# Decay attention with a softplus feed-forward block: value products of batches 1 to 7 in float32 on two column tiles

## The chip, the cores and the metric

The kernel runs on one core of a Trainium2 chip. The metric is the device time of one execution in microseconds. Three runs of the kernel before took 1167.11, 1168.81 and 1170.86 us; the median is 1168.81.

## The reference

For each of 8 batches and 8 heads there are 576 queries, keys and values of width 64, all float32, and a row of 576 forget factors f.

```python
scores = scale * np.matmul(q, k.transpose(0, 1, 3, 2))
cum = np.cumsum(np.log(np.clip(f, 0.0001, 1.0)), axis=-1)
scores = np.where(causal, -1000000000.0, scores + cum[..., :, None] - cum[..., None, :])
attn = np.exp(scores - np.max(scores, axis=-1, keepdims=True))
attn = attn / (np.sum(attn, axis=-1, keepdims=True) + 1e-09)
x = np.matmul(attn, v)          # then (B, H, S, D) -> (B*S, H*D) = (4608, 512)
h = x @ w_in                    # (512, 2048)
out = (np.maximum(h, 0.0) + np.log1p(np.exp(-np.abs(h)))) @ w_out   # (2048, 512)
```

The mask leaves a query only the keys up to its own place, so a product of the softmax with the values runs, for a group of 128 keys, over the queries from that group on.

## The kernel before

The work is a list of operations (class Plan). Each has the engines on which it may run with a cost for each, the operations that it waits for, and the buffers that it takes. Plan.run walks the list once, when the program is built: it always takes the operation that can start first by these costs, on the engine that would finish it first, and so writes out a fixed order for each engine's queue. All DMAs but a few are issued from SP's queue. A change of a cost, a buffer count or a dependence changes the whole order.

The attention is done head by head (the function attention). Batch 0 comes first, in 14 jobs of its own shapes, called plain; then 56 jobs made by whole(b, h), one for each head of batches 1 to 7. Between the units of a job, units of the feed-forward block (FFN) of earlier tokens are added, and after the last head the rest of the FFN runs alone. FFN products at L1205 (up) and L1290 (down) split each operand into a rounded high part and a low part (type float32r) and use three products for one; those of the first 256 tokens (L1186, L1309) are plain float32.

A whole job has these steps. Scores: two float32r products for each piece (L794, L795), from an operand T that four small DMAs put together. A row minimum on DVE (L799), an exponential on ACT that also sums the rows (L827), then a scaling by the reciprocal sum on ACT, POOL or DVE (L855, L857). The softmax is transposed on TensorE (L922), 128 keys by up to 512 queries in a bank of PSUM, in four banks of a head: bank 0 holds the first 64 queries against keys 0 to 63 and the last 64 queries against the last 64 keys (small), bank 1 the queries from 64 against keys 0 to 127, bank 2 those from 128 against the next 128 keys, bank 3 the rest.

Before the change, hi_part copies a bank to float32r (ph; a copy's line is L215), and lo_part subtracts that from the bank (pl, L944; L941 for the small bank, whose low part goes to partitions 64 to 127). split_v does the same to the values (vhl, cast and L723), high and low part side by side, so that one 128-column stationary operand gives both products in PSUM partitions 0 to 63 and 64 to 127. output(gi) then makes the value products (L1055): one of 64 columns for the first 64 queries, and nine for queries 64 to 575 (512, 448, 320 and 192 columns with ph and with pl, and one of 64). The two halves of the result are added in two steps: ACT copies one half into x (shift), DVE adds the other (put, L1081).

For the plain jobs there is output_tiled (L995): float32 products from one float32 copy of the transposed softmax and from V as it was loaded, with 64 stationary columns each. Each product goes to one of two column tiles of TensorE (tile_position (0, 0) or (0, 64)), which write PSUM partitions 0 to 63 and 64 to 127, and the two tiles take different ranges of queries. A float32 product is two records in the trace, one for each pass. For a rest job (one head of batch 0, queries 256 to 575) the ranges are 256 to 447 and 448 to 575.

Of the kernel before, what the change touches and what calls it, by code (L numbers as in the profile page):

```python
# [218 lines left out]
def tile_decay_attention_softplus_ffn(  # L219
# [38 lines left out]
    BUFS = dict(T=2, att=4, h=2, acc=2, fe=4, ph=3, pl=3, ph64=2, gh=LAG + 1, gl=LAG + 1, xh=1, xl=1,  # L258
                x32=2, wl=2, vhl=3, vraw=1, raw=2, one=2)
# [40 lines left out]
    PW = [64] + [128 * (i + 1) for i in range(1, 5)]  # L300
# [252 lines left out]
    def whole(b, h):  # L553


        banks = [[(0, 0, 64, 0, NCH), (512, 512, S, 0, 4)], [(0, 64, S, 0, 0)], [(128, 128, S, 0, 1)],
                 [(256, 256, S, 0, 2), (384, 384, S, 0, 3)]]
        return dict(
            b=b, heads=[h], q=(0, S), k=(0, S), nv=NCH + 1,
            tiles=[(q0, n, 0, i, 0) for i, (q0, n) in enumerate(QT)],  # L560
            banks=banks, groups=[(0, 64, h, 0), (64, S, h, 64)],
        )
# [41 lines left out]
    def attention(job):  # L604
# [33 lines left out]
        def load_v(pairs=(None,)):  # L638
            for h in pairs:
                box, vtag = {}, "vraw"  # L640
                if plain:
                    vtag = ("vhl", "vhl", "vraw", "vhl")[slot if h is None else h // 2]

                def v(e, h=h, box=box, vtag=vtag):
                    shape = [P, (NCH + 1) * (2 if vtag == "vhl" else 1), D]
                    vr = box["v"] = buf(vtag, shape, f"vr{n}")[:, 0:nv]
                    if h is not None:
                        e.dma_start(
                            out=vr[:, 0:4].rearrange("p (h c) d -> p h c d", h=2),
                            in_=vR[b, h : h + 2, :, 0:2].rearrange("h p c d -> p h c d"),  # L650
                        )
                    else:
                        e.dma_start(out=vr[:, 0:NCH], in_=vR[b, heads[0]])
# [6 lines left out]
                more = (160, 1) if plain else (192, 2)  # L660
                if h is not None:
                    more = 128, 1
                later = first_rows if plain and h is None else []
                op = add_dma(v, *more, after=later, takes=(vtag,))
                st.setdefault("vr", []).append(box)
                st.setdefault("V", []).append(op)
                st["vtag"] = vtag
                if h is not None:
                    V_of[h] = [box], [op], vtag
# [46 lines left out]
        def split_v():  # L716
            def v_hi(e):
                st["vhl"] = buf("vhl", [P, nv, 2 * D], f"vhl{n}", F32R)
                copy(e, st["vhl"][:, 0:nv, 0:D], st["vr"][0]["v"])

            def v_lo(e):
                hi, lo = st["vhl"][:, 0:nv, 0:D], st["vhl"][:, 0:nv, D : 2 * D]
                e.tensor_sub(lo, st["vr"][0]["v"], hi.bitcast(F32))  # L723

            vh = add(
                [on_act(nv * D), on_dve(nv * D, bias=COPY_BIAS)], v_hi, after=st["V"], takes=("vhl",),
            )
            vl = add(subs(nv * D), v_lo, after=[vh])
            give("vraw", [vl])
            st["V"] = [vl]  # L730

        def prepare():
# [20 lines left out]
            split_v()  # L753
# [113 lines left out]
        def weights(bi):  # L867
# [6 lines left out]
            small = spans[0][:3] == (0, 0, 64)  # L874
            blocks, need = [], []
            for ti, (q0, n_q, k0, pi, po) in enumerate(tiles):
                for key, lo, hi, _, at in spans if small else reversed(spans):
                    if q0 < hi and q0 + n_q > lo and k0 <= key:
# [6 lines left out]
                        if small:  # L885

                            x = pt[pi][:, c : c + 64]
                            one = halves
                            if key == 0:

                                x, one = x[0:68], ident[0:68, 0:68]
# [34 lines left out]

            def keep(e):
# [3 lines left out]
            more, size = ("64", P) if small else ("", 512)  # L931
            rows = 64 if small else P

            def hi_part(e):
                box["h"] = buf("ph" + more, [P, size], f"ph{n}_{bi}", F32R)[:, 0:w]
                copy(e, box["h"][0:rows], box["ps"][0:rows, 0:w])

            def lo_part(e):
                if small:
                    h = box["h"]  # L940
                    e.tensor_sub(h[64:P], box["ps"][0:64, 0:w], h[0:64].bitcast(F32))  # L941
                    return
                box["l"] = buf("pl", [P, size], f"pl{n}_{bi}", F32R)[:, 0:w]
                e.tensor_sub(box["l"], box["ps"][:, 0:w], box["h"].bitcast(F32))  # L944
# [11 lines left out]
            if plain:  # L956
                tag = tags[bi] = ("ph", "pl")[count["p"] % 2]
                count["p"] += 1
                ready = [add(on, keep, after=[m], takes=(tag,))]
                give("att", ready)  # L960
            else:
                hp = add(on, hi_part, after=[m], takes=("ph" + more,))
                ready = [hp, add(on_dve(w), lo_part, after=[hp], takes=() if small else ("pl",))]
                give("att", ready[1:])
            for key, lo, hi, vc, at in spans:
                parts.append((lo, hi, bi, vc, at, box, ready, small))

        def output_tiled():

            steps = [[] for _ in banks]  # L970
            for gi, (g0, g1, r, c0) in enumerate(groups):
                todo = [x for x in parts if x[0] < g1 and x[1] > g0]
                todo.sort(key=lambda x: (max(x[0], g0) > g0, x[2]))
                for lo, hi, bi, vc, at, pbox, ready, _ in todo:
# [3 lines left out]
                        ready=ready,  # L978
                    )
                    steps[bi].append(mm)  # L980
# [6 lines left out]
            for i, step in enumerate(steps):  # L987
# [24 lines left out]
            for r, rows, c, w, bi, o, h, tok in job["puts"]:  # L1012
# [17 lines left out]
            if quad:  # L1030
                s_of[heads[0]] = s_of[heads[2]] = st["scores"], before
            else:
                scores, reads = s_of[heads[0]] if pair else ([], [])
                give("T0", st["scores"] + scores)
                give(st["vtag"], before + reads)
# [4 lines left out]

        def output(gi):
            g0, g1, h, tok = groups[gi]
            g, j = h // 2, h % 2
            todo = sorted(
                (p for p in parts if p[0] < g1 and p[1] > g0), key=lambda p: (max(p[0], g0) > g0, p[2])
            )
            box, last = {}, []
            for i, (lo, hi, bi, vc, at, pbox, ready, small) in enumerate(todo):
                a, z = max(lo, g0), min(hi, g1)

                def values(e, i=i, a=a, z=z, vc=vc, o=at + a - lo, pbox=pbox, xs="h" if small else "hl"):
                    if i == 0:
                        box["ps"] = bank("att", f"o{n}_{gi}")
                    for x in xs:
                        e.matmul(  # L1055
                            box["ps"][:, a - g0 : z - g0], st["vhl"][:, vc[1], :],
                            pbox[x][:, o : o + z - a],
                            start=i == 0 and x == "h", stop=i == len(todo) - 1 and x == xs[-1],
                        )

                on = on_pe(z - a, len("h" if small else "hl"))
                op = add(
                    on, values, after=ready + last + st["V"],
                    takes=("att",) if i == 0 else (),
                )
                last = [op]
                used[bi].append(op)
            st.setdefault("ends", []).extend(last)
            w = g1 - g0


            def to():
                if b not in x_of:
                    x_of[b] = buf("x32", [P, NCC, S], f"x32_{b}")
                return x_of[b][64 * j : 64 * j + 64, g, tok : tok + w]

            def shift(e):
                copy(e, to(), box["ps"][64 - 64 * j : 128 - 64 * j, 0:w])

            def put(e):  # L1080
                e.tensor_add(to(), box["ps"][64 * j : 64 * j + 64, 0:w], to())  # L1081

            needs = last + x_taken.get(b, [])
            takes = () if b in x_taken else ("x32",)
            c = add(on_act(w, psum=True), shift, after=needs, takes=takes)
            d = add(on_dve(w), put, after=[c])
            x_taken.setdefault(b, [c])
            puts = [d]
            wrote.setdefault(b, []).append((tok, tok + w, d))
            give("att", puts)  # L1090
            if gi == len(groups) - 1:
                give("T", st["scores"])
                give("vhl", st["ends"])
                for bi, ops in used.items():
                    if banks[bi][0][:3] == (0, 0, 64):
                        give("ph64", ops)
# [526 lines left out]
```

## Time and profile before

| | before |
|---|---|
| runs, us | 1167.11, 1168.81, 1170.86 |
| profiled execution: span, us | 1169.7 (the page gives no other time of it) |
| TensorE (PE) busy | 1156.0 us, 99% |
| its weight loads (PEld) busy | 958.5 us, 82% |
| DVE busy | 800.1 us, 68% |
| ACT busy | 835.0 us, 71% |
| POOL busy | 136.5 us, 12% |

A group of instructions is named by its line, engine, operation and out<-in. Its busy time counts each instruction from its start to its end; matmuls are pipelined and overlap, so what a matmul takes from TensorE is read from its start to the start of the next. Idle time is shown with the instruction before which it stands and what released it. Roughly, batch 0 takes the first 130 us, the heads of batch 1 the time to 240 us, those of batches 2 to 7 the time to 980 us, and the FFN alone the rest.

### The profile page before, as it was taken

The numbers are of one execution on the slowest core, as the hardware profiler recorded it, in microseconds if no ns is written. First come the engines' busy times: TensorE is split into PE (matmuls) and PEld (weight loads), VectorE is DVE, ScalarE is ACT, GpSimd is POOL, SyncE is SP. The second block draws the span as 40 slices with busy tenths as digits, with TensorE's granted clock in tenths as the row PEclk, the third lists the DMA queues.
The fourth block names the chain that finished last, engine by engine and source line by source line (L and its number), as shares of the span: only waits on it lengthen the run. The fifth ranks groups of instructions, "written<-read, shape, count | busy, mean of one in ns | idle before, by whom it ended". The sixth has DMA issues, their size and how long they took to land.

```text
span 1169.7 us, 19392 instructions
## 1 busy us (share of the span) xinstructions
PE 1156.0 (99%) x6236; PEld 958.5 (82%) x6236; DVE 800.1 (68%) x1991; ACT 835.0 (71%) x1987; POOL 136.5 (12%) x149
## 2 busy tenths in 40 slices
PE   8999999999999999999999999999999999999998
PEld 6667788888888888888888888888888888888887
DVE  7898998987776778667876777677866772223322
ACT  6789888888867877678767786787867873444543
POOL 3323111100111101011011001110011100000000
PEclk9999999999999999999999999999999999999999
DMA  8968775555566547655566557554656433211211
GB/s 237 258 181 244 200 205 149 134 171 164 156 196 187 154 133 205 173 158 171 153 172 186 162 146 207 175 152 137 192 164 187 120 113 121 78 54 37 90 54 36
DMA packets 119397, 181.75 MB, mean 155 GB/s; under 512 B 20816, under 2 KB 78448, under 8 KB 119296
## 3 DMA queue, kind: packets, MB, share of 16 engines
q1 hardware_dynamic: 119128, 180.37, 53.3%
q8 instruction: 50, 0.82, 0.3%
q14 instruction: 51, 0.42, 0.1%
q10 hardware_dynamic: 168, 0.15, 0.0%
HBM read 110.49 MB, written 36.83 MB: 126 GB/s over the span
## 4 chain that ended last, share of the span: by engine, by line
PE 78%; DVE 9%; DMA 5%; ACT 4%; issue 2%; SPq 1%; POOL 0%; DVEq 0%; ACTq 0%; POOLq 0%
PE acc L1290 30%; PE h L1205 28%; PE b L922 7%; PE o L1055 6%; PE s L795 3%; PE s L794 3%; DMA T<-T 3%; DVE s L799 2%; ACT p L827 1%; DMA gl_5b<-g_d 1%; DVE wol_dt_float32r L538 1%; DVE xl L1157 1%; DVE woh_dt_float L470 1%; DVE vhl L723 1%; DMA sto<-in_w_out 0%
## 5 line engine op out<-in xcount | busy, mean ns | idle before, releaser
L1205 PE MATMUL h<-xh,wih 128*128 128x512 f32 (+1 forms) x576 | 229.9, 402 | 0.0
L827 ACT ACTIVATE p<-s,negm 128x288 f32<-128x288 f32 (+7 forms) x384 | 183.0, 479 | 58.0 <-DVE negm L799 53.8
L1205 PE MATMUL h<-xl,wih 128*128 128x512 f32 (+1 forms) x576 | 216.5, 379 | 0.0
L799 DVE CUSTOM_DVE_ANT_0 s<-s,cmask 128x288 f32<-128x288 f32 (+6 forms) x320 | 138.2, 438 | 90.2 <-PE s L795 83.3
L857 POOL TENSOR_SCALAR p<-p,rsum 128x448 f32<-128x448 f32 (+4 forms) x89 | 97.4, 1102 | 754.4 <-DVE rsum L841 401.4
L1252 DVE SCALAR_TENSOR_TENSOR h<-h,e 128x512 f32<-128x512 f32 x136 | 95.8, 704 | 130.1 <-ACT e L1244 129.1
L1238 ACT ACTIVATE e<-h 128x512 f32<-128x512 f32 x144 | 85.8, 596 | 119.0 <-PE h L1205 117.9
L1290 PE MATMUL acc<-woh_dt_float32r,gh 128*128 128x512 f32 x376 | 153.0, 407 | 0.0
L1205 PE MATMUL h<-xh,wl 128*128 128x512 f32 (+1 forms) x576 | 148.8, 380 | 0.0
L1290 PE MATMUL acc<-woh_dt_float32r,gl 128*128 128x512 f32 x376 | 147.3, 392 | 0.0
L1290 PE MATMUL acc<-wol_dt_float32r,gh 128*128 128x512 f32 x376 | 146.9, 391 | 0.0
L944 DVE TENSOR_TENSOR pl<-b,ph 128x512 fp32r<-128x512 f32 x168 | 111.3, 666 | 34.2 <-ACT ph L215 30.8
L215 ACT CAST ph<-b 128x512 fp32r<-128x512 f32 (+2 forms) x173 | 82.8, 482 | 56.3 <-PE b L922 51.5
L1205 PEld LDWEIGHTS h<-xh,wl 128*128 128x128 f32 x576 | 104.9, 188 | 21.6
L922 PE MATMUL b<-ident,p 128*128 128x128 f32 (+1 forms) x728 | 118.8, 269 | 2.8 <-ACT p L827 1.0
L1205 PEld LDWEIGHTS h<-xh,wih 128*128 128x128 f32 x576 | 108.8, 189 | 15.3 <-issue 0.2
L1260 DVE TENSOR_TENSOR gl<-h,gh 128x512 fp32r<-128x512 f32 x136 | 93.5, 687 | 40.2 <-ACT gh L215 39.1
L1205 PEld LDWEIGHTS h<-xl,wih 128*128 128x128 f32 x576 | 108.9, 189 | 14.4 <-issue 0.2
L922 PEld LDWEIGHTS b<-ident,p 128*128 128x128 f32 (+1 forms) x728 | 86.3, 138 | 18.8 <-ACT p L827 4.8
L215 ACT CAST gh<-h 128x512 fp32r<-128x512 f32 x114 | 66.9, 587 | 45.1 <-DVE h L1252 41.5
L794 PE MATMUL s<-T 128*64 128x64 f32 x336 | 97.3, 302 | 1.0 <-PE o L1055 0.7
L795 PE MATMUL s<-T 68*64 68x64 f32 x336 | 97.7, 295 | 0.0
(163 smaller groups left out, 2216.1 us busy)
## 6 DMA issues: line engine op xcount, KB each, us to landing
wl<-wil_d SPq DMA_DIRECT2D x72, 512.0 KB
T<-T SPq DMA_DIRECT2D x224, 144.0 KB
raw<-in_qkT SPq DMA_DIRECT2D x112, 144.0 KB
g_d<-gh SPq DMA_DIRECT2D x84, 128.0 KB
g_d<-gl SPq DMA_DIRECT2D x84, 128.0 KB
vr<-in_vR SPq DMA_DIRECT2D x64, 160.0 KB
out<-ob SPq DMA_DIRECT2D x35, 256.0 KB
sto<-in_w_out SPq DMA_DIRECT2D x11, 512.0 KB
```

Of the source, the lines that this page charges most:

```text
L215: (e.tensor_copy if hasattr(e, "tensor_copy") else e.copy)(out, in_)
L794: e.matmul(o, qA[:, q0:end], kA[:, a:z], start=True, stop=False)
L795: e.matmul(o, qB[0:ST, q0:end], kB[0:ST, a:z], start=False, stop=True)
L799: e.tensor_tensor_reduce(out=box["o"], in0=box["o"], in1=cmask[0:n_q, right - w : right], scale=-0.125, scalar=m0 if i else 3.0e38, op0=AL ...
L827: e.activation(o, box["o"], AF.Exp, bias=m1, scale=-1.0, accum_out=acc)
L857: e.tensor_scalar(a, a, f_, None, ALU.mult)
L922: e.transpose(box["ps"][0 : x.shape[1], at : at + one.shape[1]], x, one)
L944: e.tensor_sub(box["l"], box["ps"][:, 0:w], box["h"].bitcast(F32))
L1205: e.matmul(o, l, r, start=m == 0, stop=m == 11)
L1252: e.scalar_tensor_tensor(h, h, 0.0, box["e"], ALU.max, ALU.add)
L1260: e.tensor_sub(box["l"], box["t"], box["h"].bitcast(F32))
L1290: e.matmul(st["acc", tt], l, r[fc], start=first and m == 0, stop=last and m == 2,)
```

## The change

Jobs made by whole use output_tiled too. The transposed softmax is kept once, in float32 (keep), V is not split, and the queries are in two groups, 0 to 383 on the first tile and 384 to 575 on the second. The small blocks are 68 wide instead of 64, so that the products take 68 rows, of which four are zero in the softmax. The result is copied from PSUM to x in two pieces, on ACT or DVE. output, split_v, hi_part and lo_part go. Buffers: six for the transposed softmax (pt) in place of three ph and three pl, two small ones (pt64) as before, four of V (vr) in place of three vhl and one vraw.

```diff
-    BUFS = dict(T=2, att=4, h=2, acc=2, fe=4, ph=3, pl=3, ph64=2, gh=LAG + 1, gl=LAG + 1, xh=1, xl=1,
-                x32=2, wl=2, vhl=3, vraw=1, raw=2, one=2)
+    BUFS = dict(T=2, att=4, h=2, acc=2, fe=4, pt=6, pt64=2, gh=LAG + 1, gl=LAG + 1, xh=1, xl=1,
+                x32=2, wl=2, vr=4, raw=2, one=2)
...
-    PW = [64] + [128 * (i + 1) for i in range(1, 5)]
+    PW = [ST] + [128 * (i + 1) for i in range(1, 5)]
...
-        banks = [[(0, 0, 64, 0, NCH), (512, 512, S, 0, 4)], [(0, 64, S, 0, 0)], [(128, 128, S, 0, 1)],
+        banks = [[(0, 0, 64, 0, 0), (512, 512, S, 0, 4)], [(0, 64, S, 0, 0)], [(128, 128, S, 0, 1)],
...
-            banks=banks, groups=[(0, 64, h, 0), (64, S, h, 64)],
+            banks=banks, groups=[(0, 384, 0, 0), (384, S, 1, 0)],
+            puts=[(0, 384, h, 0), (64, S - 384, h, 384)],
...
-                    if nv > NCH:
-
-                        x = vR[b, heads[0], 0:64, 0]
-                        twice = bass.AP(x.tensor, x.offset, [[0, 2], *x.ap])
-                        e.dma_start(out=vr[:, NCH], in_=twice)
...
-        def split_v():
...
             def keep(e):
-                box["p"] = buf(tag, [P, 512], f"p{n}_{bi}", F32R)[:, 0:w].bitcast(F32)
-                copy(e, box["p"], box["ps"][:, 0:w])
+                rows = ST if small else P
+                box["p"] = buf(tag, [P, P if small else 512], f"p{n}_{bi}")[:, 0:w]
+                copy(e, box["p"][0:rows], box["ps"][0:rows, 0:w])
...
-                hp = add(on, hi_part, after=[m], takes=("ph" + more,))
-                ready = [hp, add(on_dve(w), lo_part, after=[hp], takes=() if small else ("pl",))]
-                give("att", ready[1:])
+            ready = [add(on, keep, after=[m], takes=(tag,))]
+            give("att", ready)
...
-                    steps[bi].append(mm)
+                    steps[bi if plain else 0].append(mm)
...
                         e.matmul(
                             box["ps"][m["r"] : m["r"] + 64, m["a"] : m["z"]],
-                            st["vr"][m["vc"][0]]["v"][:, m["vc"][1], :],
-                            m["p"]["p"][:, m["o"] : m["o"] + m["z"] - m["a"]],
+                            st["vr"][m["vc"][0]]["v"][0 : m["rows"], m["vc"][1], :],
+                            m["p"]["p"][0 : m["rows"], m["o"] : m["o"] + m["z"] - m["a"]],
                             start=m["start"], stop=m["stop"], tile_position=(0, m["r"]),
                         )
...
+            for r, w, h, tok in [] if plain else job["puts"]:
+
+                def put(e, r=r, w=w, h=h, tok=tok):
...
+                    copy(e, to, box["ps"][r : r + 64, 0:w])
...
+                on = [on_act(w, psum=True), on_dve(w)]
+                d = add(on, put, after=before + x_taken.get(b, []), takes=takes)
...
-        def output(gi):
...
-            o=[output_tiled] if plain else [lambda gi=gi: output(gi) for gi in range(len(groups))],
+            o=[output_tiled],
```

## Rows read from the trace of the kernel before

**Rows 1.** The page's part 1 with its head: busy time, share of the span and instructions of each engine.

```profile
span 1169.7 us, 19392 instructions
...
PE 1156.0 (99%) x6236; PEld 958.5 (82%) x6236; DVE 800.1 (68%) x1991; ACT 835.0 (71%) x1987; POOL 136.5 (12%) x149
```

**Rows 2.** The page's part 4, the chain of work that ended last, by engine.

```profile
PE 78%; DVE 9%; DMA 5%; ACT 4%; issue 2%; SPq 1%; POOL 0%; DVEq 0%; ACTq 0%; POOLq 0%
```

**Rows 3.** The table of stretches: from and to, length, then busy time (and instructions) of PE, PEld, DVE, ACT and POOL, the granted TensorE clock, DMA share, GB/s.

```profile
120.00:150.00 30.00, 28.92 (x183) 21.53 (x182) 28.72 (x78) 25.93 (x68) 4.20 (x3) 1.00 0.75 213
150.00:180.00 30.00, 29.36 (x194) 25.78 (x195) 27.31 (x75) 26.98 (x71) 6.37 (x5) 1.00 0.66 183
180.00:210.00 30.00, 29.09 (x189) 25.50 (x188) 26.59 (x74) 25.69 (x69) 3.54 (x3) 1.00 0.58 157
210.00:240.00 30.00, 29.77 (x183) 26.07 (x183) 27.21 (x75) 24.74 (x65) 5.45 (x5) 1.00 0.47 122
...
480.00:600.00 120.00, 120.00 (x645) 101.81 (x644) 89.85 (x223) 92.23 (x227) 12.13 (x12) 1.00 0.60 174
```

**Rows 4.** Instructions of TensorE in order of time, around the value products of two heads: start, duration, line, operation, out<-in, shape, count.

```profile
181.22 0.28 PE L1055 MATMUL o<-ph,vhl 128*128 128x64 f32 x1
181.33 0.47 PE L1290 MATMUL acc<-woh_dt_float32r,gh 128*128 128x512 f32 x1
181.65 0.39 PE L1290 MATMUL acc<-wol_dt_float32r,gh 128*128 128x512 f32 x1
181.88 0.40 PE L1290 MATMUL acc<-woh_dt_float32r,gl 128*128 128x512 f32 x1
...
272.21 0.19 PE L1055 MATMUL o<-ph,vhl 128*128 128x64 f32 x1
272.25 0.41 PE L922 MATMUL b<-halves,p 128*128 128x128 f32 x2
272.50 0.49 PE L922 MATMUL b<-ident,p 128*128 128x128 f32 x3
...
276.11 0.40 PE L1055 MATMUL o<-ph,vhl 128*128 128x512 f32 x1
...
277.47 0.28 PE L1055 MATMUL o<-pl,vhl 128*128 128x192 f32 x1
277.58 0.41 PE L1205 MATMUL h<-xh,wih 128*128 128x512 f32 x1
277.84 0.39 PE L1205 MATMUL h<-xl,wih 128*128 128x512 f32 x1
```

**Rows 5.** The same view in batch 0: FFN products without (101.06) and with (112.79) a tiled value block behind them, the block of one rest job (113.74), and the FFN products after it.

```profile
101.06 1.02 PE L1309 MATMUL acc<-wol_dt_float,g 128*128 128x512 f32 x2
101.92 1.14 PE L789 MATMUL s<-T 66*128 66x288 f32 x4
...
112.79 1.02 PE L1309 MATMUL acc<-wol_dt_float,g 128*128 128x512 f32 x2
113.74 1.31 PE L995 MATMUL o<-p,vr 128*64 128x192 f32 x18
114.98 1.98 PE L1309 MATMUL acc<-wol_dt_float,g 128*128 128x512 f32 x4
116.80 3.73 PE L1186 MATMUL h<-x,woh_dt_float 128*128 128x128 f32 x32
```

**Rows 6.** The instructions of L995: durations in ns as minimum/median/maximum, first and last start in us, the commonest shapes.

```profile
L995 PE MATMUL o<-p,vr x192: 219/273/377, 15.6 to 127.8; 128*64 128x128 f32 x112, 128*64 128x192 f32 x48, 128*64 128x64 f32 x32
```

**Rows 7.** Groups of instructions of the whole span: count, then busy us, mean ns of one, and the idle time before them with its releasers.

```profile
L944 DVE TENSOR_TENSOR pl<-b,ph 128x512 fp32r<-128x512 f32 x168 | 111.3, 666 | 34.2 <-ACT ph L215 30.8
L1081 DVE TENSOR_TENSOR x<-o,x 64x64 f32<-64x64 f32 x112 | 50.7, 452 | 12.5 <-ACT x L215 10.3 <-issue 0.2
L215 ACT COPY x<-o 64x64 f32<-64x64 f32 x112 | 44.1, 393 | 9.6 <-PE o L1055 7.0
L723 DVE TENSOR_TENSOR vhl<-vr,vhl 128x384 fp32r<-128x384 f32 x56 | 33.2, 593 | 0.7 <-ACT vhl L215 0.2
L941 DVE TENSOR_TENSOR ph<-b,ph 64x128 fp32r<-64x128 f32 x56 | 15.9, 284 | 2.8 <-ACT ph L215 1.1
L215 DVE CAST vhl<-vr 128x384 fp32r<-128x384 f32 x36 | 15.0, 416 | 0.0
L215 ACT CAST vhl<-vr 128x384 fp32r<-128x384 f32 x20 | 10.2, 512 | 5.9 <-PE o L1055 3.8 <-PE s L794 1.5 <-PE s L795 0.3
```

**Rows 8.** TensorE in order of time at a stop; in brackets the idle time and its releaser.

```profile
197.82 0.28 PE L1055 MATMUL o<-pl,vhl 128*128 128x192 f32 x1
198.76 0.21 PE L794 MATMUL s<-T 128*64 128x64 f32 x1 [0.66 <-PE o L1055]
```

**Rows 9.** Who the weight loads of TensorE waited for between 120 and 240 us: total, times, longest. The first and the last of eleven lines that name an engine or a transfer (those that name only issue are left out); the nine between have 1.0, 1.0, 0.8, 0.5, 0.4, 0.3, 0.3, 0.2 and 0.2 us.

```profile
PEld b L922 <- ACT p L827: 2.4, 4, 1.7
...
PEld b L925 <- DVE wol_dt_float32r L538: 0.2, 1, 0.2
```

**Rows 10.** What ended the idle time before the value products of the whole span (us, times), and TensorE in order of time at the longest of these stops.

```profile
  DVE x L1081: 2.6, 6
...
961.96 0.30 PE L795 MATMUL s<-T 68*128 68x288 f32 x1
962.83 0.50 PE L1055 MATMUL o<-ph,vhl 128*128 128x512 f32 x1 [0.58 <-DVE x L1081]
```

**Rows 11.** The chain of work that ended last, between 120 and 240 us, in order of time: start, us, what. The two longest transfers in it.

```profile
146.68 4.92 DMA wl<-wil_d
...
212.81 3.56 DMA T<-T
```

More of the change, by code (lines that the diff above doesn't have):

```diff
@@ L639, in load_v, with v @@
             for h in pairs:
[L640 to L646, printed above, removed]
+                box = {}
+                def v(e, h=h, box=box):
+                    vr = box["v"] = buf("vr", [P, NCH, D], f"vr{n}")[:, 0:nv]
                     if h is not None:
@@ L652, in v @@
                     else:
-                        e.dma_start(out=vr[:, 0:NCH], in_=vR[b, heads[0]])
-                    if nv > NCH:
-                        x = vR[b, heads[0], 0:64, 0]
-                        twice = bass.AP(x.tensor, x.offset, [[0, 2], *x.ap])
-                        e.dma_start(out=vr[:, NCH], in_=twice)
-                more = (160, 1) if plain else (192, 2)
-                if h is not None:
-                    more = 128, 1
+                        e.dma_start(out=vr, in_=vR[b, heads[0]])
                 later = first_rows if plain and h is None else []
-                op = add_dma(v, *more, after=later, takes=(vtag,))
+                op = add_dma(v, 160 if h is None else 128, after=later, takes=("vr",))
                 st.setdefault("vr", []).append(box)
                 st.setdefault("V", []).append(op)
-                st["vtag"] = vtag
                 if h is not None:
-                    V_of[h] = [box], [op], vtag
+                    V_of[h] = [box], [op]
         def load32():
@@ L751, in prepare @@
             low = slice(0, 64)
-            split_v()
             if number < nplain + 2:
@@ L871, in weights @@
                 w += hi - lo
-            small = spans[0][:3] == (0, 0, 64)
+            small = not plain and bi == 0
             blocks, need = [], []
@@ L925, in turn @@
                     e.transpose(box["ps"][:, at1 + at : at1 + at + m], one, ident[0:m, 0:m])
+            tag = tags[bi] = "pt64" if small else "pt"
             def keep(e):
-                box["p"] = buf(tag, [P, 512], f"p{n}_{bi}", F32R)[:, 0:w].bitcast(F32)
-                copy(e, box["p"], box["ps"][:, 0:w])
[L931 to L944, printed above, removed]
+                rows = ST if small else P
+                box["p"] = buf(tag, [P, P if small else 512], f"p{n}_{bi}")[:, 0:w]
+                copy(e, box["p"][0:rows], box["ps"][0:rows, 0:w])
             need = list(dict.fromkeys(need)) + halves_set
@@ L955, in weights @@
             on = [on_act(w, psum=True), on_dve(w)]
[L956 to L961, printed above, removed]
-                hp = add(on, hi_part, after=[m], takes=("ph" + more,))
-                ready = [hp, add(on_dve(w), lo_part, after=[hp], takes=() if small else ("pl",))]
-                give("att", ready[1:])
+            ready = [add(on, keep, after=[m], takes=(tag,))]
+            give("att", ready)
             for key, lo, hi, vc, at in spans:
-                parts.append((lo, hi, bi, vc, at, box, ready, small))
+                parts.append((lo, hi, bi, vc, at, box, ready, ST if small else P))
         def output_tiled():
@@ L973, in output_tiled @@
                 todo.sort(key=lambda x: (max(x[0], g0) > g0, x[2]))
-                for lo, hi, bi, vc, at, pbox, ready, _ in todo:
+                for lo, hi, bi, vc, at, pbox, ready, rows in todo:
                     a, z = max(lo, g0), min(hi, g1)
@@ L1011, in output_tiled @@
             puts = []
-            for r, rows, c, w, bi, o, h, tok in job["puts"]:
+            for r, w, h, tok in [] if plain else job["puts"]:
+                def put(e, r=r, w=w, h=h, tok=tok):
+                    if b not in x_of:
+                        x_of[b] = buf("x32", [P, NCC, S], f"x32_{b}")
+                    to = x_of[b][64 * (h % 2) : 64 * (h % 2) + 64, h // 2, tok : tok + w]
+                    copy(e, to, box["ps"][r : r + 64, 0:w])
+                takes = () if b in x_taken else ("x32",)
+                on = [on_act(w, psum=True), on_dve(w)]
+                d = add(on, put, after=before + x_taken.get(b, []), takes=takes)
+                x_taken.setdefault(b, [d])
+                puts.append(d)
+                wrote.setdefault(b, []).append((tok, tok + w, d))
+            for r, rows, c, w, bi, o, h, tok in job["puts"] if plain else []:
                 def put(e, r=r, rows=rows, c=c, w=w, bi=bi, o=o, h=h, tok=tok):
@@ L1029, in output_tiled @@
             give("att", puts)
-            if quad:
+            if not plain:
+                give("T", st["scores"])
+                give("vr", before)
+            elif quad:
                 s_of[heads[0]] = s_of[heads[2]] = st["scores"], before
@@ L1039, in output_tiled @@
                 give(tags[bi], ops)
-        def output(gi):
[L1042 to L1096, printed above, removed]
-                    else:
-                        give("ph", ops)
-                        give("pl", ops)
```

25 lines of the change are left out of this document (6 added, 19 removed).

## Prediction, made before the change was run

> **What bounds the kernel now.** I read the busy table first. The reader is to see that TensorE is busy for nearly the whole span while DVE and ACT have a third of theirs free [rows 1]; the chain of work that ended last is mostly TensorE too [rows 2]. A busy TensorE can still hide stops, because the ends of its matmuls are modelled, so the second view is the table of stretches [rows 3]. From 480 to 600 us TensorE is never idle and DVE is busy 89.85 of 120 us: there only TensorE work counts. From 120 to 240 us, where batch 1 runs while the weights are still being split, DVE is busy 28.72, 27.31, 26.59 and 27.21 of 30 us and TensorE is idle 1.08 + 0.64 + 0.91 + 0.23 = 2.86 us. So DVE work is worth something in that stretch only, and everywhere else the price of the change is what its value products take from TensorE. The third view is the order in time on TensorE, which gives that price from start to start.
>
> **The value products before, per head.** [Rows 4] The nine products of the large range run from 276.11 to the next start at 277.58: 1.47 us; the FFN matmul behind them takes 0.26 instead of 0.23 us to the one after, +0.03. The product of the first 64 queries stands alone: 272.21 to 272.25, 0.04, and the two transposes behind it take 0.25 where two take about 0.22, +0.03. Sum 1.57. Where an FFN matmul follows the small product instead, it is dearer: 181.22 to 181.33 is 0.11, and the next pitch is 0.32 against 0.23 (181.65 to 181.88), +0.09, sum 1.70. Both kinds occur; I take 1.60, nearer the later stage, in which most heads run, and keep 1.57 and 1.66 as ends for the mean.
>
> **The value products after, per head.** Batch 0 already runs this form, so its price is in the trace. Nine float32 products (18 records, two passes each) on two column tiles go from 113.74 to 114.98, 1.24 us [rows 5]. Two FFN matmuls ahead take 0.95 (112.79 to 113.74) instead of 0.86 (101.06 to 101.92): entry +0.09. The four behind take 1.82 (114.98 to 116.80) instead of twice 0.86: exit +0.10. So that block costs 1.43. It has, by the job's ranges, 3 x 192 + 64 = 640 columns on one tile and 4 x 128 + 64 = 576 on the other. One pass costs 273 - 219 = 54 ns per 64 columns (the shortest record is the 64-column one, the median the 128-column one) [rows 6], 0.844 ns a column; 640 columns in two passes are 1.08 us, which with start and end makes the 1.24, so the shorter tile is fully beside the longer. After the change one tile has 64 + 320 + 256 + 128 = 768 columns (queries 0 to 383), the other 4 x 192 + 64 = 832. The longer one counts: 192 columns more than in batch 0, two passes, 0.844 ns: +0.32. The block costs 1.75 us. 56 heads: (1.75 - 1.60) x 56 = +8.4 us; with the ends, 5 to 10 us. All of it lies on TensorE, and nothing covers it.
>
> A rule of the Trainium skill speaks against the side-by-side term. TensorE: Matmul & The Clock Gate (Part 3, The mechanism) says that matmuls start and end in program order with no reordering. In program order the tiles alternate, each product with both passes, and a product could start only after the one before it had started its second pass. Walking the batch 0 block through with 54 ns per 64 columns ends it at some 1.46 us (an estimate from that rule) where the row has 1.24 [rows 5], so the trace disagrees; by the rule the new block would be 0.32 us longer, which is a rival below.
>
> **What goes from DVE and ACT, per head.** [Rows 7] DVE loses three subtractions that form the low parts of the softmax, 3 x 666 ns = 2.00; the small one, 0.28; the subtraction of V, 0.59; its share of V's casts, 15.0 / 56 = 0.27; and two additions into x, 2 x 452 ns = 0.90. That is 4.04 us. ACT loses two copies into x, 2 x 393 ns = 0.79, and 10.2 / 56 = 0.18. What comes is one copy of 384 and one of 192 columns: 576 in all, as the 64 and 512 that were copied before, so 0.8 on ACT or 0.9 on DVE. The copies of the transposed softmax stay, in float32 instead of rounded. Net about 4.1 us less per head on the two engines; over the ten heads or so that begin between 120 and 240 us, some 35 us of DVE's 110 busy us go.
>
> **What that buys.** Only TensorE's stops. The lower bound of what stands in that stretch is the 2.86 us of idle. It understates: from 197.82 to 198.76 are 0.94 us, where a 192-column product takes 0.11 to the next start (277.47 to 277.58 [rows 4]), so 0.83 was lost and 0.66 is shown as idle [rows 8]. The upper bound is the wait of the weight loads on other work: eleven lines from 2.4 to 0.2 us, 7.3 us in sum [rows 9]. What is released there by ACT's exponentials and scalings and by DVE is late because DVE is full; waits for V and T transfers, and the turn from batch 0 to batch 1, stay. I take 5 us, between the two. Later in the run the stops that remain are some before value blocks: 2.6 us of idle, six times, ended by the addition into x, of which the largest is 961.96 to 962.83 [rows 10]. The addition and the low part both go, but the block still waits for the last copy out of PSUM; I take 1 us of it.
>
> **The rest.** The second transfer of V's first 64 rows goes, one issue per head on SP's queue; DMA is not what TensorE waits for in most heads, so nothing. The new first-tile width of 68 and its zero fill are one memset at the start, beside the weights' loading. The buffers of V and of the softmax are regrouped with as many as before: nothing. The one wait that the change adds is that all products of a head now stand behind all four copies as one piece. Behind it on TensorE stands whatever the list puts next, mostly FFN matmuls, which would be held for the length of a copy, about half a microsecond, if the list is wrong. In the later stage the nine ran in one piece already [rows 4], so I cost it at nothing and keep 2 us for the upper end. The list itself is worked out again from new costs, in batch 0 too, where TensorE's stops can shift either way; 1 to 2 us of that belong to the range.
>
> **Sum.** The profiled span is 1169.7 us; the page gives no other time of that execution, and it lies 0.9 above the median of the three runs and inside them. 8.4 - 5 - 1 = +2.4 us: span 1172.1, and on the median 1168.8 + 2.4 = **1171.2 us**. What is late next is TensorE alone, in batch 1 as well.
>
> **Rivals.** (1) The stops of 120 to 240 us don't go, because what comes late there is a transfer or the turn from batch 0, and DVE's load was only beside it: +8.4, up to 10 with the ends, 1177 to 1179. For it: the chain of waits of that stretch has weight and T transfers of 4.92 and 3.56 us in it [rows 11]. Against it: DVE at 96, 91, 89 and 91% just there. It decides if less than 4.9 us are won back, for then the kernel is more than 3.5 us slower. This is the rival on the other side. (2) All 7.3 and 2.6 us go, at the lower end of the price or at mine: 5 - 9.9 = -4.9, 8.4 - 9.9 = -1.5, so 1164 to 1167. For it: freed DVE time is several times the stops. Against it: some of the waits are not DVE's. (3) The products start in program order: walked through, the passes of the new block end at 1.73 us instead of 1.40, +0.32 x 56 = +18, 1189. Against it stands the 1.24 of batch 0. (4) The change doesn't do what it says, and the tiles run one after the other: (768 + 832) x 2 x 0.844 ns = 2.70 against 1.40, +1.30 x 56 = +73, 1244; the same row speaks against it.
>
> **Chances.** Forecast 0.52; rival 1 0.22; rival 2 0.21; rivals 3 and 4 together 0.05. A difference of under 0.3% (3.5 us) can't be told from none, so "same" is 1165.3 to 1172.3. Of the forecast 0.36 is same and 0.16 slower; of rival 1 0.21 slower and 0.01 same; of rival 2 0.13 faster and 0.08 same; the others are slower. Faster 0.13, same 0.45, slower 0.42. The range goes from the better half of rival 2 to rival 1's end, 1165 to 1179; the forecast's own is 1168 to 1175.
>
> **What the new profile would show.** The value line should have 18 records a head in blocks of about 1.24 + 0.32 = 1.56 us from the first start to the next instruction's, entry +0.09 and exit +0.10 as in batch 0. DVE's busy time should fall by about 200 us and its share between 120 and 240 us to two thirds; TensorE's idle time there should be under 1 us and its stops before value blocks gone. If the block is longer than 1.6 us, the tiles don't run beside each other and rival 3 or 4 holds; if the idle time there stays while DVE is free, rival 1 holds; a total outside the range would mean that the new order of the list, not these terms, sets the time.

## The result, and the profile after

The changed kernel takes 1179.03 us (median of 4 runs, 1177.4 to 1180.1) against 1169.35 (4 runs, 1167.1 to 1170.9): ratio 1.0078 [1.006, 1.0096], 9.7 us or 0.8% **slower**. Forecast were 1171.2 us, with "same" as the likeliest outcome (0.45); the time lies at the very end of the range (1165 to 1179), where rival 1 had put it, and outside the forecast's own 1168 to 1175.

The head and part 1 of the page of the changed kernel (as [rows 1]), then its part 4 (as [rows 2]):

```profile
span 1178.3 us, 19596 instructions
...
PE 1164.9 (99%) x6684; PEld 953.7 (81%) x6684; DVE 655.4 (56%) x1674; ACT 796.1 (68%) x1883; POOL 110.2 (9%) x122
...
PE 88%; DVE 5%; ACT 3%; DMA 1%; issue 1%; POOL 1%; SPq 0%; DVEq 0%; POOLq 0%; ACTq 0%
```

DVE lost 145 us of work and ACT 39, and TensorE is busy 8.9 us longer. Its idle time over the whole span, span less busy, was 13.7 us before and is 13.4 now: hardly any idle time went. The chain now runs through TensorE for 88% instead of 78%.

The table of stretches of the changed kernel (columns as in [rows 3]):

```profile
0.00:60.00 60.00, 55.58 (x342) 39.72 (x343) 45.63 (x149) 42.11 (x108) 20.75 (x40) 0.94 0.86 241
...
120.00:150.00 30.00, 27.66 (x193) 21.22 (x192) 26.97 (x73) 24.00 (x64) 2.08 (x2) 1.00 0.75 214
150.00:180.00 30.00, 29.85 (x220) 24.95 (x219) 21.20 (x64) 25.56 (x71) 4.62 (x4) 1.00 0.66 185
180.00:210.00 30.00, 30.00 (x235) 27.26 (x235) 22.40 (x66) 25.35 (x70) 4.54 (x3) 1.00 0.57 160
210.00:240.00 30.00, 30.00 (x191) 25.86 (x190) 19.61 (x52) 23.61 (x60) 1.09 (x1) 1.00 0.54 138
...
240.00:600.00 360.00, 359.90 (x2089) 298.54 (x2088) 205.44 (x537) 258.81 (x633) 28.35 (x25) 1.00 0.57 166
600.00:960.00 360.00, 359.80 (x2063) 297.69 (x2062) 198.96 (x519) 248.18 (x601) 27.02 (x25) 1.00 0.54 159
```

From 150 to 240 us TensorE's idle time fell from 0.64 + 0.91 + 0.23 = 1.78 us [rows 3] to 0.15, and DVE's share from about 90% to 70%. From 120 to 150 us the idle time rose from 1.08 to 2.34, so the whole stretch has 2.49 instead of 2.86. From 600 to 960 us it fell from 1.01 to 0.20, and in the first 60 us it rose from 3.89 to 4.42: stops went in one place and came in another. The granted clock of 0.94 in the first 60 us belongs to this execution alone: the spans of the other three are 1176.7, 1175.6 and 1177.8, so it is about 1.6 us longer than their mean.

TensorE of the changed kernel in order of time: the turn from batch 0 to batch 1, a value block in the later stage, and the last value block but one.

```profile
134.29 0.27 PE L891 MATMUL b<-halves,p 128*68 128x128 f32 x1
136.13 0.66 PE L891 MATMUL b<-ident,p 128*128 128x128 f32 x4 [1.57 <-ACT p L799]
...
401.98 1.08 PE L1112 MATMUL h<-xh,wl 128*128 128x512 f32 x4
402.99 1.64 PE L945 MATMUL o<-p,vr 68*64 68x64 f32 x18
404.55 0.50 PE L1197 MATMUL acc<-woh_dt_float32r,gh 128*128 128x512 f32 x1
404.89 0.40 PE L1197 MATMUL acc<-wol_dt_float32r,gh 128*128 128x512 f32 x1
...
970.03 1.64 PE L945 MATMUL o<-p,vr 68*64 68x64 f32 x18
972.54 0.50 PE L1197 MATMUL acc<-woh_dt_float32r,gh 128*128 128x512 f32 x1 [0.87 <-ACT gh L215]
```

The block takes 402.99 to 404.55, 1.56 us. The four matmuls ahead of it take 1.01 us instead of 4 x 0.23, entry +0.09; the one behind takes 0.34 instead of 0.23, exit +0.11. Over all heads the median is 0.091 + 1.567 + 0.108 = 1.766 us. Against the 1.60 that the prediction took for before this is +0.166 x 56 = **+9.3 us**, nearly the whole loss. Summed over the single matmuls of both traces (from start to start, and what the neighbours take beyond their usual pitch), a head takes on average 1.61 us before and 1.76 after from 240 us on, +0.15 or +8.3 for 56 heads; the products themselves are only some 0.05 us of that, the rest is entry and exit. The first two lines and the last are new stops of 1.57 and 0.87 us. The stop at 961.96 [rows 10] is gone, and this one stands in its place.

### The profile page after: what moved, and what is told of

It is laid out like the page before. It is cut to its first block, busy times and chain, and to the rows that moved or that the text cites. A ratio compares the mean times of both kernels' runs of the same rounds, so it can differ in the third digit from the quotient of the medians.

```text
span 1178.3 us, 19596 instructions
## 1 busy us (share of the span) xinstructions
PE 1164.9 (99%) x6684; PEld 953.7 (81%) x6684; DVE 655.4 (56%) x1674; ACT 796.1 (68%) x1883; POOL 110.2 (9%) x122
## 4 chain that ended last, share of the span: by engine, by line
PE 88%; DVE 5%; ACT 3%; DMA 1%; issue 1%; POOL 1%; SPq 0%; DVEq 0%; POOLq 0%; ACTq 0%
PE acc L1197 32%; PE h L1112 31%; PE b L891 8%; PE o L945 7%; PE s L767 3%; PE s L766 3%; PE acc L1216 1%; ACT p L799 1%; DVE s L771 1%; PE h L1093 1%; POOL p L829 1%; PE s L761 1%; DMA sti<-in_w_in 1%; DMA T<-in_qkT 1%; DVE wol_dt_float32r L538 0%
## 5 line engine op out<-in xcount | busy, mean ns | idle before, releaser
L829 POOL TENSOR_SCALAR p<-p,rsum 64x64 f32<-64x64 f32 (+4 forms) x62 | 69.8, 1134 | 784.9 <-DVE rsum L813 400.7
L215 ACT CAST gh<-h 128x512 fp32r<-128x512 f32 x132 | 77.5, 587 | 74.0 <-DVE h L1159 59.0
L945 PEld LDWEIGHTS o<-p,vr 128*64 128x64 f32 (+1 forms) x1200 | 88.6, 137 | 28.8 <-issue 6.8
L945 PE MATMUL o<-p,vr 128*64 128x192 f32 (+5 forms) x1200 | 107.6, 316 | 0.2 <-ACT p L215 0.2
L215 DVE COPY p<-b 128x512 f32<-128x512 f32 (+3 forms) x120 | 62.9, 535 | 69.2 <-PE b L891 67.6
```

The lines of the kernel that those rows point to most:

```text
L215: (e.tensor_copy if hasattr(e, "tensor_copy") else e.copy)(out, in_)
L829: e.tensor_scalar(a, a, f_, None, ALU.mult)
L945: e.matmul(box["ps"][m["r"] : m["r"] + 64, m["a"] : m["z"]], st["vr"][m["vc"][0]]["v"][0 : m["rows"], m["vc"][1], :], m["p"]["p"][0 : m["r ...
```

## Experiments

The theory was: the price per head lies all on TensorE, and the relief of DVE is worth a few us. The rival: the relief is worth nothing. A second question was what the price consists of. Each kernel was timed beside the kernel before on the same chip. The times are medians; the ratios are taken over all runs of both, and can differ by a tenth of a per cent from that of the medians.

**The tiled form in batch 1 only.** The kernel before, with the changed path chosen by a flag (its code is that of the change):

```
+        tiled = b == 1
+            banks=banks, groups=[(0, 384, 0, 0), (384, S, 1, 0)] if tiled else [(0, 64, h, 0), (64, S, h, 64)],
...
-            if plain:
+            elif plain or tiled:
```

> The kernel before, with the tiled float32 value products in the 8 heads of batch 1 only, the stretch in which DVE was full; batches 2 to 7 as before. Theory (each tiled head costs TensorE 1.766 - 1.60 = 0.17 us, and freeing DVE buys back some 3 us of stops in batch 1): 8 x 0.17 - 3 = -1.6, so 1167.7. Rival (the freed DVE time buys nothing, the stops of that stretch are the turn from batch 0): +1.4, 1170.7.

Measured: 1170.87 us, ratio 0.9997 [0.9985, 1.001], so -0.3 us between -1.8 and +1.2. Its table of stretches, and TensorE in order of time at the turn:

```profile
120.00:150.00 30.00, 27.41 (x191) 20.48 (x190) 26.99 (x73) 22.96 (x64) 3.73 (x3) 1.00 0.72 206
150.00:240.00 90.00, 89.85 (x622) 78.15 (x622) 67.73 (x191) 76.04 (x200) 9.87 (x7) 1.00 0.60 166
```

```profile
131.29 0.27 PE L926 MATMUL b<-halves,p 128*68 128x128 f32 x1
133.12 0.66 PE L926 MATMUL b<-ident,p 128*128 128x128 f32 x4 [1.56 <-ACT p L831]
```

The theory's 3 us didn't come. Eight heads cost 8 x 0.166 = 1.3 us, so 1.6 us were won back (0.1 to 3.1 by the interval), where 5 had been forecast. Some of that never showed as idle time: summed as above, a head of 130 to 240 us took 1.88 us in the kernel before, with short stops inside and beside its block, and 1.75 in the changed one. Otherwise the picture is that of the full change: the idle time of 150 to 240 us goes (0.15 us are left), and a stop of 1.56 us, which waits for ACT's exponentials, appears at the turn.

**The tiled form in batches 2 to 7 only.**

```
+        tiled = b >= 2
```

> The kernel before, with the tiled products in batches 2 to 7 only (48 heads). Theory (a price per head, nothing bought where TensorE never stops): 48 x 0.17 = +8.0, so 1177.3, with blocks of 1.77 us as in the changed kernel. Rival (the loss is an accident of the list's new order in batch 1 and at the turn): under +4, below 1173.

Measured: 1178.65 us, 1.0065 [1.0046, 1.0085], +7.6 us between +5.4 and +9.9; 48 x 0.166 = 8.0, and 48 x 0.15 = 7.2. The price per head is borne out where TensorE had hardly any stops to lose (1.15 us of idle from 240 to 960 us before).

**Before without its low parts.** This takes DVE's work away and leaves TensorE's as it was.

```
-                ready = [hp, add(on_dve(w), lo_part, after=[hp], takes=() if small else ("pl",))]
+                ready = [hp]
...
-                            pbox[x][:, o : o + z - a],
+                            pbox["h"][:, o : o + z - a],
...
-            d = add(on_dve(w), put, after=[c])
+            d = c
```

> The kernel before without the low parts of the three large softmax banks and without the last addition into x; the products read the high part twice, so TensorE has the same matmuls. It leaves out part of the sum. DVE loses 2.0 + 0.9 us a head. Theory (freed DVE time is worth about 3 us of stops in all): 1166 to 1167. Rival 1 (it is worth the 6 us that the prediction took): 1163. Rival 2 (it is worth nothing): 1169.

Measured: 1169.16 us, 0.9997 [0.9974, 1.0019], so -0.3 us between -3.0 and +2.2 (by the medians -1.3). DVE's busy time fell to 669.9 us. Its table of stretches, and a stop later in its run:

```profile
120.00:150.00 30.00, 29.48 (x185) 22.18 (x185) 28.39 (x83) 26.06 (x70) 5.78 (x4) 1.00 0.74 214
150.00:180.00 30.00, 29.54 (x202) 26.06 (x200) 23.97 (x67) 27.59 (x74) 2.56 (x3) 1.00 0.73 203
180.00:210.00 30.00, 29.80 (x204) 26.95 (x204) 22.39 (x68) 27.09 (x74) 5.16 (x4) 1.00 0.60 163
210.00:240.00 30.00, 30.00 (x174) 26.10 (x173) 20.61 (x57) 22.97 (x59) 2.60 (x2) 1.00 0.53 148
```

```profile
719.07 0.21 PE L794 MATMUL s<-T 128*64 128x64 f32 x1 [1.53 <-issue]
```

Idle time of 120 to 240 us is 0.52 + 0.46 + 0.20 = 1.18 us instead of 2.86, so in place the relief does what was said. But stops stand elsewhere, one of them of 1.53 us, and over the whole span idle time is 1165.4 - 1152.1 = 13.3 us, against 13.7 before. The likely cause is that the list of operations is worked out again from the new costs; this is argued, since no run kept the old order. The same work taken from DVE, without the tiles, is worth no time that can be measured, 3 us at most.

**The changed kernel with DVE's work put back.** Three spare subtractions from PSUM and one of V per head, which hold the buffers as the old ones did. Of the 4.0 us per head that DVE lost, 2.6 are put back.

```
+                def spare(e):
+                    e.tensor_sub(spare_[:, 0:w], box["ps"][:, 0:w], box["p"])
+
+                extra = add(on_dve(w), spare, after=ready)
+                give("att", [extra])
```

> The changed kernel with the removed DVE work put back as dummies that no product waits for: three subtractions from PSUM (which hold their banks as before) and one of V's size a head, 2.6 us of DVE. Theory (freed DVE time is worth about 3 us of stops): +2 to +3, so 1181 to 1182. Rival (it is worth nothing): 1179.

Measured: 1183.62 us, 1.0106 [1.0083, 1.013], 0.28% or 3.3 us above the changed kernel's 1.0078; the two intervals overlap. Its table of stretches, and what TensorE waited for most (total, times, longest):

```profile
120.00:150.00 30.00, 29.47 (x198) 21.80 (x196) 29.09 (x75) 23.88 (x64) 5.34 (x4) 1.00 0.75 220
150.00:240.00 90.00, 88.70 (x625) 76.54 (x626) 75.23 (x207) 74.27 (x198) 11.71 (x8) 1.00 0.57 158
240.00:600.00 360.00, 358.52 (x2074) 296.54 (x2071) 249.73 (x625) 254.26 (x625) 32.77 (x29) 1.00 0.57 165
600.00:960.00 360.00, 358.44 (x2055) 296.61 (x2054) 245.60 (x608) 242.01 (x589) 31.34 (x28) 1.00 0.54 157
...
PE b L897 <- POOL p L835: 2.3, 5, 0.5
```

Idle time of 240 to 960 us is 1.48 + 1.56 = 3.04 us, where the changed kernel has 0.10 + 0.20. In this kernel DVE's work is felt in the late stage, where I had not put it; five of the stops, 2.3 us of all, wait for a scaling on POOL. It is felt from 150 to 240 us too, as I had put it: idle time is 1.30 us there instead of 0.15. In return the stop at the turn is not in this run (120 to 150 us: 0.53 instead of 2.34).

**One more switch of tiles.** A full-array product of 128 columns with zero weights in the middle of each block.

```
+                            e.matmul(box["ps"][:, 0:P], cmask[:, 0:P], ident, start=False, stop=False)
```

> The changed kernel with one product of the full array in the middle of each value block (weights of zeros, 128 float32 columns, added to results already begun), so each head leaves the two tiles and enters them once more. Theory (leaving and entering cost 0.09 + 0.10 + 0.09 + 0.05 us beside the product's own 0.22): +0.55 a head, +31 over the changed kernel, about 1210. Rival (the switch costs nothing and a tiled head is dear for its passes alone): +12, about 1191.

Measured: 1204.88 us, 1.0298 [1.0285, 1.0312]: 0.0220 x 1170, some 26 us above the changed kernel. TensorE in order of time at one block:

```profile
754.14 0.39 PE L1199 MATMUL acc<-woh_dt_float32r,gl_3b 128*128 128x512 f32 x1
754.46 0.87 PE L947 MATMUL o<-p,vr 68*64 68x64 f32 x8
755.26 0.49 PE L946 MATMUL o<-ident,cmask 128*128 128x128 f32 x2
755.67 0.99 PE L947 MATMUL o<-p,vr 128*64 128x256 f32 x10
756.59 0.50 PE L1199 MATMUL acc<-woh_dt_float32r,gh_4b 128*128 128x512 f32 x1
```

The block takes 0.80 + 0.41 + 0.92 = 2.13 us instead of 1.57. Of the extra 0.56 the product itself is 2 x 128 x 0.844 ns = 0.22, so leaving the tiles and coming back costs 0.34 us. 0.56 x 56 is the 31 of the theory; 5 us less were measured. Idle time over the span accounts for 1.4 of that (1202.4 - 1190.4 = 12.0 us; the late stop of 0.87 us is 0.30 here); the rest is not placed. The rival's price is excluded.

**The tiles listed one after the other.**

```
-                step = [m for ms in zip_longest(*sides) for m in ms if m]
+                step = [m for ms in (sides if not plain else zip_longest(*sides)) for m in ms if m]
```

> The changed kernel with the products of a head listed tile by tile, all four of the first and then all five of the second, in place of alternating. If the tiles start from one queue in program order, or look ahead by only a few, the second waits for most of the first: block up to 1.30 + 1.40 + 0.16 = 2.86 us instead of 1.57, up to +73, 1252. If each tile takes its own products whatever the order: the block stays at 1.57 and the time at 1179.

Measured: 1213.14 us, 1.037 [1.0354, 1.0385], some 34 us above the changed kernel: neither theory. TensorE in order of time, and the instructions of this block that had started by 412.66, by shape:

```profile
411.94 2.34 PE L945 MATMUL o<-p,vr 68*64 68x64 f32 x18
414.21 0.50 PE L1197 MATMUL acc<-woh_dt_float32r,gh 128*128 128x512 f32 x1
...
L945 PE MATMUL o<-p,vr x6: 222/378/435, 411.9 to 412.7; 68*64 68x64 f32 x2, 128*64 128x320 f32 x2, 128*64 128x256 f32 x1, 128*64 128x192 f32 x1
```

The block is 2.27 us. Fully side by side it is 1.57, one after the other 1.57 + 1.30 = 2.87. The 0.70 more are 0.05 more than the first two products of the first tile take (64 + 320 columns, two passes, 0.844 ns: 0.65). The last line shows the same: the second tile's first record (192 columns) starts together with the first record of the first tile's third product (256 columns), while that product's second record and both of the fourth (128 columns) are still to come. So the second tile starts ahead of products that stand before it in the list, but not of all of them: here it passed three waiting records and no more. Whether the matmul is held back or the load of its weights, this run doesn't tell.

**Two heads in one block**, so that the tiles are entered and left once for two heads; the second head's ranges are exchanged between the tiles, which makes 768 + 832 = 1600 columns on each. Six and two buffers of the softmax become eight and four.

```
-            banks=banks, groups=[(0, 384, 0, 0), (384, S, 1, 0)],
+            banks=banks, groups=[(0, 384, h % 2, 0), (384, S, 1 - h % 2, 0)],
...
+                if heads[0] % 2 == 0:
+                    held[0] = values, need, cols, lambda op: finish_whole(op, box)
+                    return
+                first_, need0, cols0, finish0 = held.pop(0)
...
+                op = add(cost, both, after=need0 + need, takes=("att", "att"))
```

> The changed kernel with the value products of two heads of a batch made in one block and the second head's ranges on exchanged tiles, so that each tile has 768 + 832 = 1600 columns and the switch is paid once for two heads; 8 buffers for the softmax in place of 6. Theory (the price is the switch and the longer tile): 1600 x 2 x 0.844 ns + 0.33 = 3.03 us for two heads, 1.52 each instead of 1.77: -14 against the changed kernel, 1165, and 4 below the kernel before. Rival (the loss comes from the list's order): at most -4, 1175 or more.

Measured: 1173.43 us, 1.0031 [1.0014, 1.0048]. TensorE in order of time, at a turn between batches, a block and the end; and the table of stretches:

```profile
321.56 0.41 PE L766 MATMUL s<-T 128*128 128x320 f32 x1 [0.98 <-ACT p L799]
...
395.85 1.08 PE L1136 MATMUL h<-xh,wl 128*128 128x512 f32 x4
396.86 2.94 PE L966 MATMUL o<-p,vr 68*64 68x64 f32 x36
399.73 0.50 PE L1221 MATMUL acc<-woh_dt_float32r,gh 128*128 128x512 f32 x1
400.07 0.39 PE L1221 MATMUL acc<-wol_dt_float32r,gh 128*128 128x512 f32 x1
...
962.62 0.50 PE L1221 MATMUL acc<-woh_dt_float32r,gh 128*128 128x512 f32 x1 [2.44 <-ACT gh L215]
```

```profile
240.00:600.00 360.00, 357.07 (x2098) 300.65 (x2095) 199.88 (x528) 262.21 (x637) 24.26 (x25) 1.00 0.57 167
600.00:960.00 360.00, 357.68 (x2086) 300.63 (x2084) 197.94 (x518) 258.94 (x626) 25.79 (x25) 1.00 0.54 158
```

A block costs 0.09 + 2.87 + 0.11 = 3.07 us, against 2 x 1.766 = 3.53: 28 x 0.46 = 12.9 us less. Measured are 0.0047 x 1170 = 5.5. Most of the rest stands in the rows: idle time of 240 to 960 us is 2.93 + 2.32 = 5.25 us instead of 0.30, and the late stop is 2.44 instead of 0.87.

**The same without the exchange** (1536 and 1664 columns).

```
-            banks=banks, groups=[(0, 384, h % 2, 0), (384, S, 1 - h % 2, 0)],
+            banks=banks, groups=[(0, 384, 0, 0), (384, S, 1, 0)],
```

> The same with the ranges on the same tiles for both heads (1536 and 1664 columns), so that the switch alone is saved. Theory: 1664 x 2 x 0.844 ns + 0.33 = 3.14 us for two heads, 1.57 each: -11 against the changed kernel, 1168; the exchange of tiles is worth the other 3.

Measured: 1176.46 us, 1.0065 [1.0041, 1.0089], 3.0 us above the one with it by the medians; 64 columns x 2 x 0.844 ns x 28 = 3.0. The medians agree with the price of the longer tile; the intervals overlap.

**Two heads in a block, with the FFN work spread otherwise.** The stops at the turns say that too little FFN work is left there: the rule that shares it out between the heads gets a larger divisor.

```
-        share = sum(c for c, _ in ffn) / (until - n + 1 + DELAY) / max(1, len(units))
+        share = sum(c for c, _ in ffn) / (until - n + 1 + (2 if n < nstart else 2.65)) / max(1, len(units))
```

> Two heads a block with exchanged tiles as before, and the units of the FFN spread over a little more of the attention after batch 0 (the number that is added to the remaining jobs is 2.65 in place of 2), so that some are left where the scores stood still at each turn of a batch (1 us near 320, 448, 576, 704 and 832 us, 2.6 near 960). Theory (the block is paid as measured, 3.08 us for two heads, and what was lost beside it was lack of other work there): 8 less than two heads a block, 1165 to 1167, faster than the kernel before by 3 to 5. Rival (the scores stand still for PSUM banks that the larger block holds): the stops stay, 1173.

Measured: 1167.32 us, 0.9966 [0.9954, 0.9978]: 4 us **faster than the kernel before**, and the fastest of all. TensorE in order of time at the same turn; the table of stretches, and what TensorE waited for most from 600 to 960 us:

```profile
320.46 2.94 PE L966 MATMUL o<-p,vr 68*64 68x64 f32 x36
323.34 0.24 PE L766 MATMUL s<-T 128*64 128x64 f32 x1
```

```profile
240.00:600.00 360.00, 359.18 (x2103) 300.60 (x2103) 188.84 (x515) 268.02 (x664) 25.00 (x23) 1.00 0.58 167
600.00:960.00 360.00, 357.10 (x2091) 298.70 (x2091) 187.31 (x494) 263.08 (x642) 25.16 (x21) 1.00 0.53 156
...
PE acc L1221 <- DMA gl_5b<-g_d: 2.4, 2, 1.4
```

The stop at 320 us is gone, which speaks against the rival, and idle time of 240 to 600 us is 0.82 us. From 600 to 960 us it is 2.90, of which 2.4 are two stops that wait for transfers of the split hidden layer. Over the whole span it is 14.1 us instead of 19.8.

**The changed kernel with its FFN work spread so** (the same line with 2.5).

> The changed kernel with the same spreading alone (2.5 in place of 2). Theory (the changed kernel lost by its blocks and not for lack of other work; its stop of 0.9 us near 971 may go): -1, about 1178. Rival (the spread of the FFN was what cost it the time): 1172 or less.

Measured: 1178.03 us, 1.0055 [1.0042, 1.0067]; the changed kernel has 1.0078 [1.006, 1.0096], so 1.0 us less by the medians, 2.7 by the ratios, and the intervals overlap. Its page, and its stretches at the turn and at the end:

```profile
span 1175.8 us, 19644 instructions
...
PE 1163.4 (99%) x6684; PEld 952.7 (81%) x6684; DVE 619.5 (53%) x1643; ACT 811.3 (69%) x1921; POOL 105.3 (9%) x115
...
120.00:150.00 30.00, 28.77 (x205) 21.91 (x204) 26.64 (x77) 24.80 (x71) 4.40 (x3) 1.00 0.82 225
960.00:1160.00 200.00, 200.00 (x915) 165.51 (x914) 57.07 (x87) 88.44 (x151) 1.41 (x1) 1.00 0.21 70
```

The spread alone is no cure: from 240 to 960 us the changed kernel was idle for 0.30 us, and there was nothing to win. Both of the changed kernel's new stops are gone here, that of 1.57 us at the turn (the longest from 120 us on is 0.70) and that of 0.87 us at the end. Idle time over the span is still 12.4 us instead of 13.4, since others came, and the kernel is still 0.55% slower than the one before. What makes the version above fast is the block of two heads, and the spread keeps its gain from being lost in stops.

## Where the prediction was right and where it failed, point by point

**What bounds the kernel**: right. Only TensorE's path counts; 145 us less of DVE bought no time that can be told from none.

**The value products after**: right. 1.75 us were forecast from batch 0's rows, 1.766 measured; block 1.56, entry 0.09 and exit 0.10 were 1.567, 0.091 and 0.108. Before, 1.60 is borne out by the 1.61 from 240 us on; in batch 1 it was 1.88. The forecast +8.4 is +8.3 to +9.3, and the runs of batch 1 alone (-0.3) and of the rest (+7.6) add up, within their intervals, to what the whole change costs.

**What goes from DVE and ACT**: right per operation, too large in sum. 4.1 us per head are 230 us; DVE and ACT lost 145 + 39 = 184. From 120 to 240 us DVE lost 20 us, where some 35 were forecast. DVE took over work: its copies of the transposed softmax are 62.9 us where casts and copies were 30.6 + 8.7, and its scaling is 25.9 where it was 10.3, some of that taken from POOL, which lost 26 us. Line groups of the changed kernel:

```profile
L215 DVE COPY p<-b 128x512 f32<-128x512 f32 (+3 forms) x120 | 62.9, 535 | 69.2 <-PE b L891 67.6 <-PE b L894 0.9
...
L829 DVE TENSOR_SCALAR p<-p,rsum 128x576 f32<-128x576 f32 (+2 forms) x41 | 25.9, 632 | 0.9
```

**"I take 5 us, between the two", and 1 us later: this is the step that failed.** Idle time in place was read rightly as DVE's: with DVE freed, 150 to 240 us lost 1.63 of 1.78 us, and the stop at 961.96 went. But I took a stop that goes for time won. In the new list a stop of 1.57 us stands at the turn from batch 0 and one of 0.87 us at the end; the total stayed, 13.7 and 13.4 us, and where another list had neither of the two (the spread alone), it was 12.4. Relief alone (before without low parts) was worth 0.3 us by the ratio, 3 at most; in batch 1 with the tiles 1.6. The upper bound by the waits of weight loads [rows 9] was far above what any run won back (3.1 us at most). The prediction had the sentence that the list is worked out again, and priced it at 1 to 2 us of either sign in the range; the stops that came, whatever put them there, took back nearly all that the old ones gave. That the total still lies within the range is owed to rival 1, up to whose end the range was drawn, and not to the sum.

**Rival 1** gave the right time, 1177 to 1179, and half the right mechanism: "the turn from batch 0" is indeed what is late in 120 to 240 us. Its other half, that stops stay because of transfers, is not what the rows show; those stops went. Its sign, idle time that stays from 120 to 240 us, was there: 2.49 us where under 1 was forecast. **Rival 2** is excluded by the same runs. **Rival 3** gave a block of 1.56 + 0.32 = 1.88 us; with the products alternating the trace has 1.567. The rule of the Trainium skill (TensorE: Matmul & The Clock Gate, Part 3, The mechanism) that matmuls start in program order does not hold here. The instructions that had started by 404.03 in the block shown above are these:

```profile
L945 PE MATMUL o<-p,vr x13: 222/326/435, 403.0 to 404.0; 128*64 128x192 f32 x7, 68*64 68x64 f32 x2, 128*64 128x320 f32 x2, 128*64 128x256 f32 x2
```

The seventh record of 192 columns belongs to the second tile's fourth product, and none of the first tile's 128-column product, which the list has before it, is there yet. Listed tile by tile the block is 2.27 us, so the order of the list does count, only not strictly. **Rival 4** (one tile after the other, 1.30 us more a block) is excluded by the 1.567.

What stays open: why the list with tiles in batch 1 puts a stop at the turn, while the list without low parts does not. That it is the new order that moves the stops fits all runs but is not shown, for no run had the new work in the old order.

## What to carry to other kernels

Price a changed piece of the bounding engine from start to start, with entry and exit, at a place where the form already runs: that was 1% off here. Idle time that goes in one place is not time won while a list is made anew from costs: count it only up to what an experiment with that work simply left out returns, here nothing that can be told. Where a change of tiling has a fixed price per block, put two blocks together and balance the tiles, and then look at the stops again: that turned +0.8% into -0.3%.

## What was not expected of the hardware

How far two column tiles run beside each other depends on the order of the list: with the four products of one ahead of the five of the other, the block is 2.27 us, and alternating it is 1.57. Entering and leaving the tiled form costs 0.20 us of a 1.77 us block in its neighbours' time alone, and one more switch in the middle 0.34 us besides the 0.22 of the product that makes it.
